# Where the exponential's table is loaded, an empty step among merged work, and the order of the last product's halves

## The chip, the cores and the metric

The kernel runs on one core of a Trainium2 chip. The metric is the device time of one execution in microseconds; lower is better. The core has five engines that run side by side, each with its own list of instructions: TensorE (PE, matrix products; its weight loads are listed as PEld), VectorE (DVE), ScalarE (ACT, the engine that evaluates functions from tables), GpSimd (POOL) and SyncE (SP, which here only issues transfers). ScalarE also issues some transfers; in the profile "SPq" and "ACTq" are those issues.

## The reference

Eight batches; each goes through attention with two separate softmaxes, a two-dimensional Fourier transform of which the real part is added, a layer norm, and a two-layer network, all in float32.

```python
# q, k, v: (8 batches, 8 heads, 576 rows, 64 columns)
q_s = exp(q - max(q, axis=-1)); q_s = q_s / (sum(q_s, axis=-1) + 1e-09)      # over the columns of a head
k_s = exp(k - max(k, axis=2));  k_s = k_s / (sum(k_s, axis=2) + 1e-09)       # over the rows
kv = np.einsum('bhsd,bhse->bhde', k_s, v)
x = np.einsum('bhsd,bhde->bhse', q_s, kv)          # then (B, S, H*D) = (8, 576, 512)

mixed = np.real(fft(fft(x, axis=1), axis=2))
u = x + mixed
un = (u - mean(u)) / np.sqrt(var(u) + 1e-06)
return u + np.maximum(un @ w_ch1, 0.0) @ w_ch2     # w_ch1: 512 x 2048, w_ch2: 2048 x 512
```

## The kernel before

**Groups and orders.** The rows of a batch that aren't handled as its own 512 (64 a batch) are collected over all batches in a ninth "shared" group of 512 rows. The two-layer network runs over the nine groups in the order 0 to 6, 8 (shared), 7. "Order" below means the place in that list, 0 to 8. Order 0 is done by plain products (`plain`). Orders 1 to 8 use Strassen's seven products in place of eight, for the first layer (`up`, L850) and the second (`down`, L886). Each of these is 112 products of 128x128 by 128x256, so 224 main products to an order.

**What runs between the main products.** While the network runs for one group, all the earlier work of the next batch runs in between. `merged(main, side)` deals the side steps out evenly among the main steps:

- Among the `up` of order n: the attention of batch n + 1. `k_exp` takes the maximum (L455, VectorE) and the exponential (L457, ScalarE), `k_turn` transposes on TensorE (L467, L474; copies to `ks` at L468 and L476), `k_times_v` multiplies (L484). `q_exp` does the same for `q` (L519, L521, normalised at L526), `q_turn` and `t_turn` transpose it (L532), `q_times_kv` multiplies (L564), and ScalarE copies the result to `x` (L566 and L581).
- Among the `down` of order n: the Fourier transform of batch n + 1, in four fold steps on VectorE and GpSimd (L603 to L625) and five blocks of products (L655, L658); then two mixing steps for the batch's own rows, a third for the shared rows of a pair of batches when the batch is odd (products L678 and L681, sums into x at L696 and L697); then seven steps of the next group's norm.

**The norm.** Statistics on VectorE (L726, L727), the square root on ScalarE (L730), its reciprocal and the mean's product on VectorE (L731, L732), then four normal rows on ScalarE (L744), each followed by a transpose on TensorE (L750) and a copy to `unT` (L754). ScalarE's tables for the exponential and the square root are different ones, and the program loads one ahead of the first instruction that needs it: exponentials (L457, L521) run in each `up`, the root at the end of each `down`. In orders 6 and 7 there is no attention left.

**Strassen's ends.** A product's result lies in a bank named `ba`, `bb` or `bc`; VectorE sums at L818, L822 and L861, ScalarE applies the relu at L862, GpSimd forms the sums of operands of the second layer from it (L341 to L344). The operands are formed from `unT` in the same way (L348 to L350).

**Weights.** `used(n)` is called behind the last product with a weight block and issues the load of block n + 4 on SP's queue (L392 for the first layer, L394 for the second), so weights stream in with three or four blocks ahead.

**The tail.** In the last group (`last`, order 8) the second layer's last two products, m = 4 and m = 3, are summed by halves: `sums` adds a half of the bank (L903) to x and calls `store`. Half i = 0 is stored through ScalarE's queue, half i = 1 through SP's. A chunk for which the row half and the column half of the group agree (c == u) is stored directly (L935); any other is mirrored, first to a scratch tile in DRAM (L939), then from there in reverse order to the output (L941). For m = 4 the mirrored one is i = 0, for m = 3, the last, it is i = 1.

The instructions of each engine are put in their final order by a scheduler, from the program's order and from what each instruction needs, not by the text alone.

Of the kernel before, what the change touches and what calls it, by code (L numbers as in the profile page):

```python
# [40 lines left out]
F32 = mybir.dt.float32  # L41
I32, U32 = mybir.dt.int32, mybir.dt.uint32
ACT = mybir.ActivationFunctionType
# [3 lines left out]
P = 128  # L47
# [75 lines left out]
class _Block:  # L123
# [466 lines left out]
    def transform(self, b):  # L590


        nc, V, G = self.nc, self.nc.vector, self.nc.gpsimd
        Z = self.work.tile([P, KT, HD], F32, tag="Z", name="Z", bufs=1)
        self.Z[b] = Z
        x = {(c, u): self.xpart(b, c, u) for c in range(2) for u in range(2)}
        eo = {}

        def tokens_folded(some=range(4)):
            for i in some:  # L600
                e, op = ((V if b == 0 else G), ALU.add) if i < 2 else (V, ALU.subtract)
                eo[i] = self.halves()
                e.tensor_tensor(out=eo[i][:, 0:D], in0=x[i % 2, 0], in1=x[i % 2, 1], op=op)  # L603

        def columns_folded(some=range(4)):
            for i in some:
                e, op = ((V if b == 0 else G), ALU.add) if i < 2 else (V, ALU.subtract)
                t = eo[i]
                e.tensor_tensor(out=t[:, 1:HD], in0=t[:, 1:HD], in1=t[:, D - 1:HD:-1], op=op)
                if b == 0:  # L610
                    self.warm(t[:, 0:HD], 2)

        def by_frequency(some=range(4)):

            for i in some:
                e, op = ((G, ALU.add), (G, ALU.subtract), (V, ALU.add), (V, ALU.subtract))[i]
                one, two = eo[i // 2 * 2], eo[i // 2 * 2 + 1]
                (V if b == 0 else e).tensor_tensor(out=eo[i][:, NN:], in0=one[:, 0:NN], in1=two[:, 0:NN], op=op)

        def columns_again(some=(2, 3, 0, 1)):  # L620

            for i in some:
                t, y = eo[i], eo[i][:, NN:]
                V.tensor_tensor(out=t[:, 0:QD], in0=y[:, 0:QD], in1=y[:, HD:QD:-1], op=ALU.subtract)
                V.tensor_tensor(out=y[:, 0:QD], in0=y[:, 0:QD], in1=y[:, HD:QD:-1], op=ALU.add)  # L625

        def at_first():

            for some in ((2, 3), (0, 1)):
                for f in (tokens_folded, columns_folded, by_frequency, columns_again):  # L630
                    f(some)

            t = self.small.tile([P, 1], F32, tag="root", name="root", bufs=1)
            V.tensor_scalar(out=t[:], in0=eo[1][:, NN:NN + 1], scalar1=0.0, scalar2=None, op0=ALU.mult)
            nc.scalar.activation(t[:], t[:], ACT.Sqrt)
            self.wait_for(eo[1][:, NN:], [self.raws[i] for i in range(4)])

        def block(k):


            g = self.live["g", b]
            sines = k in (2, 3)
            own = slice(*{0: (NN, NN + QD), 4: (NN + QD, NN + QD + 1), 1: (0, QD), 2: (NN + 1, NN + QD + 1),
                          3: (1, QD)}[k])
            tail = slice(*{0: (0, QD), 4: (QD, QD + 1), 1: (NN, NN + QD), 2: (1, QD + 1), 3: (NN + 1, NN + QD)}[k])
            n = own.stop - own.start
            if k == KT:

                own, tail = slice(own.start, own.start + P), slice(tail.start, tail.start + P)
            full = self.acc((own.stop - own.start, 512))  # L650
            pz = full[0:n]
            f = sines * NM
            for odd, at, size in ((1, 0, MO), (0, MO, ME)):
                t = eo[3 - odd if sines else odd]
                nc.tensor.matmul(full[:, at:at + size], lhsT=t[:, own], rhs=self.ft[:, f + at:f + at + size], start=at == 0,  # L655
                                 stop=False, skip_group_check=True)
            f += 2 * NM
            nc.tensor.matmul(full[:, 0:NM], lhsT=g[:, tail], rhs=self.ft[:, f:f + NM], start=False, stop=True,  # L658
                             skip_group_check=True)
            z, zt = (self.Zr[0:1], self.ZTr[0:1]) if k == KT else (Z[0:n, k, :], self.ZT[0:n, k, :])  # L660
            nc.scalar.copy(paired(z), interleaved(pz[:, NT - 1:NT - 1 + 2 * ME])[:, 0:P, :])

            at = W * (b % 2)
            nc.scalar.mul(paired(zt[:, at:at + Q]), interleaved(pz[:, 0:2 * MO])[:, 0:NT - 1, ::-1],
                          -1.0 if sines else 1.0)
            nc.scalar.copy(paired(zt[:, at + Q:at + W]), interleaved(pz[:, 0:2 * ME])[:, NT - 2::-1, ::-1])

        folds = [tokens_folded, columns_folded, by_frequency, columns_again] if b else [at_first]
        return folds + [lambda k=k: block(k) for k in (2, 3, 0, 1, 4)]

    def second(self, z, zr, add):

# [43 lines left out]
    def norm(self, g):  # L716

        nc, V = self.nc, self.nc.vector
        mv = self.small.tile([P, 4, 2], F32, tag="mv", name="mv", bufs=2)
        std = self.small.tile([P, 4], F32, tag="std", name="std", bufs=2)  # L720
        unT = self.work.tile([P, 7, 2, HD], F32, tag="unT", name="unT", bufs=1)
        uns = {}

        def stats(i):
            st = self.small.tile([P, 6], F32, tag="st", name="st", bufs=2)
            V.bn_stats(st[:], self.xpart(g, i % 2, i // 2))  # L726
            V.bn_aggr(mv[:, i, :], st[:])  # L727

        def scales(s):
            nc.scalar.activation(std[:, s], mv[:, s, 1], ACT.Sqrt, bias=self.eps[:, 0:1])  # L730
            V.reciprocal(std[:, s], std[:, s])  # L731
            V.scalar_tensor_tensor(out=mv[:, s, 0], in0=mv[:, s, 0], scalar=-1.0, in1=std[:, s], op0=ALU.mult,  # L732
                                   op1=ALU.mult)

        def normal(i):
            un = self.halves()
            x = self.xpart(g, i % 2, i // 2)
            if g == 0:
                V.tensor_scalar(out=un[:, 0:D], in0=x, scalar1=std[:, i:i + 1], scalar2=mv[:, i, 0:1], op0=ALU.mult,
                                op1=ALU.add)  # L740
                if i == 1:
                    self.wait_for(un, [self.raws[i] for i in range(4, 11)])
            else:
                nc.scalar.activation(un[:, 0:D], x, ACT.Identity, bias=mv[:, i, 0:1], scale=std[:, i:i + 1])  # L744
            uns[i] = un

        def turn(i):
            pt = self.turned()
            for k in range(KT):
                nc.tensor.transpose(pt[:, k, :], uns[i][:, k * P:(k + 1) * P], self.ident[:])  # L750

            c, u = i % 2, i // 2
            cols = slice(c * P, (c + 1) * P)
            nc.scalar.copy(unT[:, u:u + 3:2, :, cols], pt[:].rearrange("p (a k) t -> p a k t", a=2))  # L754

        def all_stats():

            for some in ((0, 2), (1, 3)) if g == 0 else (range(4),):
                for i in some:
                    stats(i)  # L760
                scales(slice(some[0], 4, some[1] - some[0]))

        def combine():
            if g > 0:
                self.b_side(lambda i: unT[:, i], lambda i: unT[:, i], V, nc.gpsimd, V)

        return unT, [all_stats] + pipelined((0, 2, 1, 3), [normal, turn]) + [combine]
# [107 lines left out]
    def down(self, g, at):  # L875
        nc, V = self.nc, self.nc.vector
# [3 lines left out]
        def product(m, bank, first, final):  # L880
            n = 15 * at + NP + ORDER.index(m)

            def run(i, q):
                w = self.stream[n]
                for p in range(4 * q, 4 * q + 4):
                    nc.tensor.matmul(bank()[:, i, :], lhsT=h[p][:, A_AT[m], i * P:(i + 1) * P], rhs=w[:, p, :],  # L886
                                     start=first and i == 0 and p == 0, stop=p == NP - 1,
                                     skip_group_check=True)
                if (i, q) == (1, 1):
                    self.used(n)  # L890
                if last and m in (4, 3) and q == 1:
                    sums(m == 4, m != 4, bank(), i)
            return [lambda i=i, q=q: run(i, q) for i in range(2) for q in range(2)]

        def early(i, j, t):
            u, d = i - 1 if (i, j) != (1, 2) else 0, j - 1
# [48 lines left out]
def kernel(ctx: ExitStack, tc: tile.TileContext, q, kT, v, w1, w2, ft,  # L945
# [4 lines left out]
    def front(b, loads=None):  # L950

        first = blk.attention(b, loads)
        steps = late(lambda: blk.transform(b), 9 if b else 6)
        mixes = [lambda c=c: blk.mix_own(b, c) for c in range(2)]
        if b % 2:

# [136 lines left out]
```

## Time and profile before

| what | value |
|---|---|
| median of 8 runs | 1142.64 us (1141.52 to 1145.96) |
| the profiled execution, its own time | 1145.96 us |
| its span | 1144.2 us |
| TensorE's mean granted clock | 0.992 |
| TensorE busy | 1102.2 us, 5472 instructions |
| ScalarE busy | 397.9 us, 956 instructions |
| GpSimd busy | 332.5 us |
| table loads at L457 (exponential) | 7, 1283 ns each |
| table loads at L730 (root) | 7, 1283 ns each |
| other table loads | 2 (L229 at the start, L635 in order 0) |

Times are from the start of the span. Order 0 ends at 204.5 us, orders 1 to 6 at 329.7, 450.5, 574, 694.6, 818.7 and 940, order 7 at about 1046; the last product ends at 1136.9. A line of the timeline gives start, duration, engine, line, operation, output <- inputs, and in brackets how long the engine was idle before it and what it then waited for. Neighbouring instructions of one line are shown as one (x4). One main product is two passes through the array and counts as two instructions.

### The profile page before, as it was taken

The numbers are of one execution on the slowest core, as the hardware profiler recorded it, in microseconds if no ns is written. First come the engines' busy times: TensorE is split into PE (matmuls) and PEld (weight loads), VectorE is DVE, ScalarE is ACT, GpSimd is POOL, SyncE is SP. The second block draws the span as 40 slices with busy tenths as digits, with TensorE's granted clock in tenths as the row PEclk, the third lists the DMA queues.
The fourth block names the chain that finished last, engine by engine and source line by source line (L and its number), as shares of the span: only waits on it lengthen the run. The fifth ranks groups of instructions, "written<-read, shape, count | busy, mean of one in ns | idle before, by whom it ended". The sixth has DMA issues, their size and how long they took to land.

```text
span 1144.2 us, 14639 instructions
## 1 busy us (share of the span) xinstructions
PE 1102.2 (96%) x5472; PEld 922.0 (81%) x5472; DVE 544.3 (48%) x1110; ACT 397.9 (35%) x956; POOL 332.5 (29%) x302
## 2 busy tenths in 40 slices
PE   5799899989999999999999999999999999999997
PEld 5644455878888988888889888788889888888886
DVE  6784766378334734385335633583334352202301
ACT  6585433374133612371226322541234132201200
POOL 2075442235003510324024402261034213302320
PEclk8999999999999999999999999999999999999999
DMA  9377595454346434544356326552454344444451
GB/s 312 116 242 258 210 307 166 137 199 150 106 148 228 180 138 144 182 164 170 129 177 219 148 102 188 180 199 106 143 185 153 111 151 162 183 139 154 150 184 55
DMA packets 92549, 193.79 MB, mean 169 GB/s; under 512 B 23088, under 2 KB 59696, under 8 KB 85312
## 3 DMA queue, kind: packets, MB, share of 16 engines
q1 hardware_dynamic: 90680, 191.82, 49.1%
q10 hardware_dynamic: 1800, 1.05, 0.3%
q8 instruction: 43, 0.70, 0.2%
q14 instruction: 26, 0.21, 0.1%
HBM read 168.72 MB, written 28.31 MB: 172 GB/s over the span
## 4 chain that ended last, share of the span: by engine, by line
PE 79%; DVE 10%; ACT 5%; DMA 3%; issue 1%; POOL 1%; SPq 0%; ACTq 0%; POOLq 0%; DVEq 0%
PE bb L850 13%; PE bb L886 13%; PE bc L886 10%; PE bc L850 9%; PE ba L850 8%; PE ba L886 8%; PE acc L484 3%; PE acc L564 2%; PE bc L789 2%; PE acc L655 2%; PE acc L658 2%; PE tr L467 1%; PE acc L678 1%; PE tr L750 1%; PE tr L532 1%
## 5 line engine op out<-in xcount | busy, mean ns | idle before, releaser
L850 PE MATMUL bb<-unT,big 128*128 128x256 f32 x768 | 188.0, 381 | 0.6 <-DVE u L822 0.6
L886 PE MATMUL bb<-big 128*128 128x256 f32 x768 | 172.8, 379 | 0.0
L850 PEld LDWEIGHTS bb<-unT,big 128*128 128x128 f32 x768 | 142.7, 190 | 24.7 <-DVE u L818 3.4
L886 PEld LDWEIGHTS bb<-big 128*128 128x128 f32 x768 | 145.1, 190 | 20.0
L341 POOL TENSOR_TENSOR big<-big 128x512 f32<-128x512 f32 (+1 forms) x38 | 45.1, 1188 | 310.4 <-ACT big L862 305.7
L850 PE MATMUL bc<-unT,big 128*128 128x256 f32 x512 | 125.2, 379 | 0.0
L850 PE MATMUL ba<-unT,big 128*128 128x256 f32 x512 | 124.3, 379 | 0.0
L862 ACT ACTIVATE big<-big 128x512 f32<-128x512 f32 x96 | 60.3, 628 | 171.0 <-DVE big L861 170.7
L886 PE MATMUL bc<-big 128*128 128x256 f32 x512 | 116.5, 379 | 0.5 <-DVE x L903 0.5
L886 PE MATMUL ba<-big 128*128 128x256 f32 x512 | 114.1, 379 | 0.0
L886 PEld LDWEIGHTS bc<-big 128*128 128x128 f32 x512 | 95.9, 190 | 14.2 <-DVE x L903 0.9
L886 PEld LDWEIGHTS ba<-big 128*128 128x128 f32 x512 | 95.9, 190 | 12.3
L850 PEld LDWEIGHTS bc<-unT,big 128*128 128x128 f32 x512 | 95.5, 190 | 12.5
L850 PEld LDWEIGHTS ba<-unT,big 128*128 128x128 f32 x512 | 95.0, 190 | 11.7
L822 DVE TENSOR_TENSOR u<-bb,s 128x512 f32<-128x512 f32 x40 | 27.6, 690 | 134.8 <-PE bb L886 79.5
L521 ACT ACTIVATE q<-q,qm 128x64 f32<-128x64 f32 x240 | 61.6, 338 | 10.7 <-DVE qm L519 9.9
L349 POOL TENSOR_TENSOR unT<-unT 128x512 f32<-128x512 f32 x8 | 14.2, 1774 | 173.1 <-DVE unT L348 173.1
L818 DVE TENSOR_TENSOR u<-bb,s 128x512 f32<-128x512 f32 x40 | 27.6, 691 | 76.8 <-PE bb L850 38.1
L898 POOL TENSOR_TENSOR x<-x,u 128x512 f32<-128x512 f32 x14 | 17.7, 1268 | 148.6 <-DVE u L822 118.3
L861 DVE TENSOR_TENSOR big<-bc,u 128x512 f32<-128x512 f32 x64 | 44.1, 689 | 26.7 <-PE bc L850 25.9
L814 ACT COPY s<-ba 128x512 f32<-128x512 f32 x40 | 23.4, 584 | 90.0 <-PE ba L886 46.2
L754 ACT COPY unT<-tr 128x512 f32<-128x512 f32 x36 | 20.6, 585 | 86.5 <-PE tr L750 86.0
(221 smaller groups left out, 1665.0 us busy)
## 6 DMA issues: line engine op xcount, KB each, us to landing
big<-w1s SPq DMA_DIRECT2D x64, 896.0 KB
big<-w2s SPq DMA_DIRECT2D x56, 1024.0 KB
big<-in_w_dram SPq DMA_DIRECT2D x21, 512.0 KB
k<-in_kT_dram SPq DMA_DIRECT2D x26, 288.0 KB
q<-in_q_dram SPq DMA_DIRECT2D x27, 256.0 KB
v<-in_v_dram SPq DMA_DIRECT2D x26, 256.0 KB
words<-in_w_dram SPq DMA_DIRECT2D x11, 512.0 KB
w2s<-big SPq DMA_DIRECT2D x8, 512.0 KB
```

The source lines that it names most:

```text
L341: e1.tensor_tensor(out=to(4), in0=at(2), in1=at(3), op=ALU.add)
L484: nc.tensor.matmul(pk, lhsT=ks[:, c, :], rhs=v[:, c, :], start=(c == 0), stop=(c == NC - 1))
L521: nc.scalar.activation(heads[:, h, :], heads[:, h, :], ACT.Exp, bias=m[:, h:h + 1])
L564: nc.tensor.matmul(px[:, r * P:(r + 1) * P], lhsT=qT[:, r, :], rhs=self.kvr[b % 2][:, r, :], start=True, stop=True)
L655: nc.tensor.matmul(full[:, at:at + size], lhsT=t[:, own], rhs=self.ft[:, f + at:f + at + size], start=at == 0, stop=False, skip_group_chec ...
L814: nc.scalar.copy(temp("s1"), box["ba"][:])
L818: V.tensor_tensor(out=temp("u2"), in0=box["bb"][:], in1=box["s1"][:], op=ALU.add)
L822: V.tensor_tensor(out=temp("u3"), in0=box["bb"][:], in1=box["s1"][:], op=ALU.add)
L850: nc.tensor.matmul(bank()[:, i, :], lhsT=w[:, WA_AT[m], k * P:(k + 1) * P], rhs=unT[:, B_AT[m], k, :], start=first and i == 0 and k == 0, ...
L861: V.tensor_tensor(out=hp(i), in0=bank[:], in1=u[:], op=ALU.add)
L862: nc.scalar.activation(hp(i), hp(i), ACT.Relu)
L886: nc.tensor.matmul(bank()[:, i, :], lhsT=h[p][:, A_AT[m], i * P:(i + 1) * P], rhs=w[:, p, :], start=first and i == 0 and p == 0, stop=p == ...
```

## The change

Three edits.

1. In the norms of all groups but the first, behind the root, the reciprocal and the product: a one-column tile `root` gets the exponential of the root's first column (scale 0). Its value isn't used; it is an instruction that needs the exponential's table.
2. Between the four fold steps and the five blocks of the transforms of batches 2 to 7, an empty step. `merged` deals out one step more.
3. In the last product of the last group the halves run in the order 1, 0, so the mirrored chunk is summed and stored first; `used` follows the second of them.

```diff
@@ transform
         folds = [tokens_folded, columns_folded, by_frequency, columns_again] if b else [at_first]
-        return folds + [lambda k=k: block(k) for k in (2, 3, 0, 1, 4)]
+
+        return folds + [lambda: None] * (b > 1) + [lambda k=k: block(k) for k in (2, 3, 0, 1, 4)]
@@ norm, scales
             V.scalar_tensor_tensor(out=mv[:, s, 0], in0=mv[:, s, 0], scalar=-1.0, in1=std[:, s], op0=ALU.mult,
                                    op1=ALU.mult)
+            if g > 0:
+
+                t = self.small.tile([P, 1], F32, tag="root", name="root", bufs=1)
+                nc.scalar.activation(t[:], std[:, 0:1], ACT.Exp, scale=0.0)
@@ down
         def product(m, bank, first, final):
             n = 15 * at + NP + ORDER.index(m)
 
+            order = (1, 0) if last and m == 3 else (0, 1)
+
             def run(i, q):
...
-                if (i, q) == (1, 1):
+                if (i, q) == (order[1], 1):
                     self.used(n)
                 if last and m in (4, 3) and q == 1:
                     sums(m == 4, m != 4, bank(), i)
-            return [lambda i=i, q=q: run(i, q) for i in range(2) for q in range(2)]
+            return [lambda i=i, q=q: run(i, q) for i in order for q in range(2)]
@@ front
-        steps = late(lambda: blk.transform(b), 9 if b else 6)
+        steps = late(lambda: blk.transform(b), (6, 9, 10)[min(b, 2)])
```

## The prediction

> **What bounds the kernel now.** I read the page's busy shares first, then TensorE's list of waits (whole, then stage by stage), then the timeline around the waits that the change can reach.
>
> ```profile
> span 1144.2 us, 14639 instructions
> PE 1102.2 (96%) x5472; PEld 922.0 (81%) x5472; DVE 544.3 (48%) x1110; ACT 397.9 (35%) x956; POOL 332.5 (29%) x302
> ```
>
> TensorE is busy 96% of the span, so only what stops TensorE, or lies behind its last product, can be won or lost. Neither the empty step nor the table loads touch its work: 1102.2 us stay. What stops it (us in total, times, longest):
>
> ```profile
> PE acc L484 <- ACT ks L468: 9.6, 7, 4.1
> PE tr L467 <- ACT k L457: 3.5, 3, 1.5
> PE tr L532 <- DVE q L526: 2.2, 3, 1.3
> ...
> PE acc L655 <- DVE eo L625: 0.7, 2, 0.5
> ```
>
> Taken by stretches of time, all but 0.4 us of L484 falls into order 0 (before 204 us), which has no Strassen stage. From 204 us on the waits are few: L467 1.47 in order 1, 1.04 in each of orders 3 and 5; L532 2.2, all in order 1; L655 0.2 in order 5 and 0.54 in order 6. Orders 2 and 4 show none. One L467 wait in the timeline (start, duration, engine; the bracket is the idle time before it):
>
> ```profile
> 233.03 0.74 DVE L455 TENSOR_REDUCE km<-k 128x1 f32<-128x576 f32 x1
> ...
> 233.15 0.63 ACT L862 ACTIVATE big<-big 128x512 f32<-128x512 f32 x1 [1.10 <-DVE big L861]
> ...
> 233.79 1.28 ACT L457 ACT_TABLE_LOAD   x1
> ...
> 235.09 0.78 ACT L457 ACTIVATE k<-k,km 128x576 f32<-128x576 f32 x1
> ...
> 236.01 0.66 PE L467 MATMUL tr<-ident,k 128*128 128x128 f32 x4 [1.47 <-ACT k L457]
> ```
>
> The maximum is ready at 233.77 and ScalarE is free at 233.78; the load stands between that and the exponential, and TensorE waits for the exponential. Where the load would go instead:
>
> ```profile
> 315.10 0.30 ACT L730 ACTIVATE std<-mv,eps 128x4 f32<-128x4 f32 x1 [4.31 <-DVE mv L727]
> 315.56 0.17 DVE L731 RECIPROCAL std<-std 128x4 f32<-128x4 f32 x1
> 315.76 0.17 DVE L732 SCALAR_TENSOR_TENSOR mv<-mv,std 128x4 f32<-128x4 f32 x1
> 315.96 2.22 ACT L744 ACTIVATE eo<-x,mv,std 128x512 f32<-128x512 f32 x3 [0.56 <-DVE mv L732]
> ...
> 317.56 0.60 PE L750 MATMUL tr<-ident,eo 128*128 128x128 f32 x4
> ```
>
> ScalarE idles only 0.56 us there before the normals (L744) that TensorE's transposes (L750) need. Last, the tail, the queues and sums only:
>
> ```profile
> 1132.67 0.42 DVE L903 TENSOR_TENSOR x<-bc,x 128x256 f32<-128x256 f32 x1 [2.16 <-PE bc L886]
> ...
> 1133.56 0.63 ACTq L941 DMA_DIRECT2D out_dram<-mirror  x1
> 1136.91 0.42 DVE L903 TENSOR_TENSOR x<-bc,x 128x256 f32<-128x256 f32 x1 [3.81 <-PE bc L886]
> 1137.40 0.33 SPq L939 DMA_DIRECT2D mirror<-x  x1
> 1139.11 0.67 SPq L941 DMA_DIRECT2D out_dram<-mirror  x1
> ```
>
> The span ends 5.1 us after the last issue: the last chunk is stored twice in a row, through `mirror`.
>
> **The change part by part.** Besides the text I use the built order of instructions on each engine, before and after. It shows that the scheduler moves far more than the diff does. Places are counted in main products (L850 up, L886 down), 224 to an order; one takes two passes of 0.216 us (3.45 us for 16 passes), so 0.43 us.
>
> *Table loads.* Of seven L457 loads one stays (batch 1); eight loads and eight `root` exponentials come behind the square roots. 16 loads become 19: ScalarE gets 3 × 1.28 + 8 × 0.20 (the `root` row of L229) = 5.5 us more. ScalarE is busy 35%, so the sum costs nothing by itself; the place does. The norms of the last two groups load a table that no later exponential uses, one of them with a second switch behind it.
>
> *Attention in orders 3 and 5.* L467 starts 1.21 us later than TensorE's pace allows (482.15 against 480.08 + 4 × 0.216), the following L484 0.35, the next L467 about 0.3: 1.86 us. Without the load the exponential starts 1.30 us earlier, so the first delay goes. L484 now stands one product nearer to its L467 and waits 0.35 + 0.43 = 0.78 for the copy of `ks`; the next pair moves three products (1.30 us) on and waits no more. Gain 1.86 - 0.78 = 1.08 in each order, 2.1 in both (0 to 3.7).
>
> *Attention in order 1.* L467's delay is 1.63 (236.01 against 233.95 + 2 × 0.216). It moves two products earlier: 1.63 - 1.30 + 0.86 = 1.19 stay, gain 0.44. Four L532 are delayed by 0.77, 0.21, 0.46 and 1.48, in all 2.92. The five L532 move behind by 5, 4, 2, 4 and 6 products (0.9 to 2.6 us), more than each delay; but one load of `q` on SP's queue also moves behind a load of `w2s` (1 MB), and the exponentials of `q` move on ScalarE. If `q`'s chain stays, 2.92 are won; if it moves as far, nothing. I take half, 1.46. Order 1: -1.9 (+0.5 to -3.4; the upper end is that late load of `q`).
>
> *Empty step.* In even orders the first block (L655) moves from product 140 to 144, 1.73 us later; in order 6 it is delayed 0.70 us, behind L625, and that goes: -0.7. Orders 2 and 4 have nothing to win there. In odd orders the first block stays at 144, where the folds on VectorE have only 0.1 to 0.3 us in hand, so I give back 0.5 of the attention's gains there. All later blocks and one to three of the mixes (L678) move by four products.
>
> *Normals.* A load and a `root`, 1.28 + 0.20, stand between square root and normals, with 0.56 us of idle time to swallow them: normals about 1.0 us later in odd orders (0.9 if all the idle time serves, 1.5 if none does), 0.8 in even ones (0.82 idle at 436.07). In odd orders the first transpose moves from product 200 to 207 (3.0 us). In order 1 its slack was 0.8 (317.56 against 315.96 and 0.81 for one normal); 0.8 + 3.0 - 1.0 = 2.8, from which up to 2.4 goes because VectorE now takes an output sum (L911, 0.66) and the mixes' rows, moved by 1.73 us, ahead of the last statistics. It stays above nothing by some 0.3. In even orders the transposes don't move (slack 3.1 in order 2), against 0.8 for the load and 1.7 for the mixes: 0.3 to 0.6 left. So no wait, narrowly. Order 5 waits 0.54 for its first normal today, which I count as 0.3 won (0.5 lost to 0.5 won).
>
> *Borders of the orders.* In orders 1, 3 and 5 the last transpose moves from product 220 to 224, directly ahead of the next order's first product, as in even orders today. There the first `bb` group runs 0.23 us longer, so +0.7 for three. At the end of order 0 normals and transposes move too: +0.2.
>
> *Tail.* The mirrored chunk goes first, its two stores lie under the second half of the product. The last sum (to 1137.33) is then followed by one plain store, L935, on ScalarE's queue. But that queue holds L941 of the product before behind it (today at 1133.56), and that order is unchanged: L935 at 1137.40 takes 0.34, L941 goes at about 1137.8 and needs the same 5.1 us, so the end is at 1142.8: -1.4. With that L941 out of the way it would be about -4; the lower bound is 0.
>
> Sum: -2.1 - 1.9 + 0.5 - 0.7 - 0.3 + 0.7 + 0.2 - 1.4 = -5.0 us. The profiled execution took 1145.96 (span 1144.2, 1.8 around it), the slowest of the eight shown; it would go to 1141.0. Taken from their median, 1142.64, it gives 1137.6.
>
> *A rule against it.* The trace shows 1.28 us for a load, with 0.02 us on either side of it. The Trainium skill ("ScalarE: Activation LUTs", "What ACT_TABLE_LOAD costs") puts a drain of about 1.38 us to each load, about 2.66 for a switch, and its rules ask for fewer switches, where this change makes three more. By that price, an estimate, normals would be 1.4 us later than above, and six orders would wait some 0.9 us each, 5 to 6 in all, which would take the whole gain.
>
> **The rivals.**
>
> *The folds keep the gains (chance 0.17).* What attention wins is lost again at the first block of orders 1, 3 and 5, since VectorE's folds set its start. For it: L655 waits for L625 in order 5 already. Against: the folds start from sums that TensorE's L564 feeds, so they come earlier too. Left: tail -1.4, order 6 -0.7, borders +0.9, order 5 -0.3: -1.5, 1141.1.
>
> *Normals late (0.15; the slower side).* Square root and normals slip past the slack of 0.3 to 0.6, at the first transposes of orders 1 to 6: VectorE runs one more row of a mix (0.74 + 0.15 + 0.42 + 0.42 = 1.73, the rows at 432.42 to 433.89) ahead of the last statistics than I placed. Price 6 × (1.73 - 0.45) = 7.7, so 1145.3. It outweighs the rest when normals come 0.45 + 5.0 / 6 = 1.3 us later than worked out. For it: the slack is thin and VectorE's order is the scheduler's. Against: VectorE is idle for much of these stretches and the built order shows the rows that I counted.
>
> *All waits go (0.08).* Order 1 wins 3.4, orders 3 and 5 all 3.7, the folds follow: 3.6 more, 1134.0. Against: L484 behind its own L467.
>
> **How the numbers follow.** The forecast has 0.60. Faster means by over 0.2% (2.3 us, about what a measurement of this kernel can tell from no change): nearly all of the forecast (0.57), all of the last rival (0.08), a little of the first (0.02): 0.67. Same: most of the first rival, a little of the forecast and of the second: 0.20. Slower: the second, 0.13. The forecast's own range is 1136.1 to 1140.0, with order 1 at its bounds (1.5 down, 2.4 up). The range given reaches down to the third rival and up past the first, 1134.0 to 1142.2, and leaves out the second and a little below.
>
> **What would show it.** L467's waits on `k` after 204 us gone in orders 3 and 5, near 1 us in order 1; L484 waiting 0.8 us in orders 3 and 5; L532's waits under 1.5 us; L655's gone in order 6; no L750 wait on L744 above 0.5; the last issue an L941 on ScalarE's queue at 5 us before the end. Wrong would be: L750 in the list of waits with several us, new waits at L655 in odd orders, or at `bb` L850 behind a border.

## The result and the profile after

The changed kernel takes 1138.1 us (median of 14 runs, 1135.5 to 1143.46) against 1143.01 us before (38 runs, 1141.43 to 1146.02): a ratio of 0.9957, 95% interval 0.9948 to 0.9966, so 4.9 us faster. Its profiled execution took 1141.34 us with a span of 1139.5. The forecast was 5.0 us. That the sum came out so close is partly luck: three of its terms were right to a tenth of a microsecond, the two largest were too large by about 2.5 together, and what I had given back to the folds was a gain. The sections below take them apart.

Lines below the edits are shifted: the up products are L855 now (L850 before), the down products L893 (L886), the root L731 (L730), the table load and exponential behind it L738, normals L749 (L744), their transposes L755 (L750), the last sums L910 (L903), the stores L942, L946 and L948 (L935, L939, L941).

First TensorE's waits over the whole changed run (us in total, times, longest):

```profile
PE acc L484 <- ACT ks L468: 9.3, 6, 3.5
...
PE tr L532 <- DVE q L526: 3.9, 3, 2.0
...
PE tr L467 <- ACT k L457: 1.1, 1, 1.1
...
PE tr L532 <- PE bb L855: 0.6, 1, 0.6
PE bc L893 <- DVE x L910: 0.5, 1, 0.5
...
PE tr L532 <- DVE T L554: 0.5, 1, 0.5
```

L467's waits fell from three to one, L655's on the folds are gone, and the wait on L749's normals is gone too. But L532's waits on q rose from 2.2 to 3.9, where the prediction had named under 1.5 as a sign of being right. Order 3's attention shows the intended part (start, duration, engine, line; the bracket is idle time):

```profile
478.29 0.74 DVE L455 TENSOR_REDUCE km<-k 128x1 f32<-128x576 f32 x1
...
478.41 0.63 ACT L867 ACTIVATE big<-big 128x512 f32<-128x512 f32 x1 [1.10 <-DVE big L866]
479.07 0.78 ACT L457 ACTIVATE k<-k,km 128x576 f32<-128x576 f32 x1
...
480.07 0.60 PE L467 MATMUL tr<-ident,k 128*128 128x128 f32 x4
...
481.40 1.27 PE L484 MATMUL acc<-v,ks 128*128 128x128 f32 x9 [0.62 <-ACT ks L468]
```

The exponential follows the relu at once, and L467 has no bracket: its wait is gone. L484 pays in part, as it stands right behind L467 now. The load is here instead (norm at the end of order 1):

```profile
315.14 0.30 ACT L731 ACTIVATE std<-mv,eps 128x4 f32<-128x4 f32 x1 [3.73 <-DVE mv L728]
315.45 1.28 ACT L738 ACT_TABLE_LOAD   x1
...
316.75 0.20 ACT L738 ACTIVATE root<-std 128x1 f32<-128x1 f32 x1
316.86 2.21 ACT L749 ACTIVATE eo<-x,mv,std 128x512 f32<-128x512 f32 x3
319.47 0.60 PE L755 MATMUL tr<-ident,eo 128*128 128x128 f32 x4
```

From the root's start to the first normal it is 1.72 us, before 0.86. The first normal ends near 317.66 (316.86 and 0.80), 1.8 us ahead of its transpose. The tail, sums and queues:

```profile
1129.45 0.42 DVE L910 TENSOR_TENSOR x<-bc,x 128x256 f32<-128x256 f32 x1 [2.17 <-PE bc L893]
...
1131.65 0.67 SPq L948 DMA_DIRECT2D out_dram<-mirror  x1
1133.69 0.42 DVE L910 TENSOR_TENSOR x<-bc,x 128x256 f32<-128x256 f32 x1 [3.81 <-PE bc L893]
1134.19 0.34 ACTq L942 DMA_DIRECT2D out_dram<-x  x1
1134.58 0.63 ACTq L948 DMA_DIRECT2D out_dram<-mirror  x1
```

The last issue is the mirrored store of the product before, on ScalarE's queue behind the plain one. The span, 1139.54, ends 5.0 us after it, and 5.85 us after the last sum's start (before: 1144.16 - 1136.91 = 7.25).

The table lists how long each up and each down took in the profiled executions, from the start of its first main product to that of the next part. "Untouched" is the third experiment below, whose instructions before the last product are those of the kernel before; it shows which differences are scatter. Orders 7 and 8 and the downs of orders 2 and 4 are the same in all, to 0.02 us. (Order 7 ends at 1039.2 us before, not at 1046.)

| part | before | untouched | after | after - before | exponential alone | empty step alone |
|---|---|---|---|---|---|---|
| order 0 ends at | 204.49 | 200.02 | 203.90 | -0.59 | 203.44 | 200.24 |
| order 1 up | 67.93 | 68.04 | 67.44 | -0.49 | 67.43 | 67.91 |
| order 1 down | 57.26 | 57.25 | 57.23 | -0.03 | 57.23 | 57.25 |
| order 2 up | 62.35 | 62.35 | 62.59 | +0.24 | 62.35 | 62.58 |
| order 3 up | 66.16 | 65.32 | 66.15 | -0.01 | 64.86 | 65.43 |
| order 3 down | 57.23 | 57.62 | 57.23 | 0.00 | 57.24 | 57.52 |
| order 4 up | 62.35 | 62.35 | 62.59 | +0.24 | 62.35 | 62.59 |
| order 5 up | 65.88 | 65.46 | 64.85 | -1.03 | 64.81 | 65.68 |
| order 5 down | 58.24 | 58.11 | 57.23 | -1.00 | 57.23 | 57.63 |
| order 6 up | 62.35 | 62.35 | 62.59 | +0.24 | 62.35 | 62.59 |
| order 6 down | 59.12 | 59.13 | 58.35 | -0.77 | 59.13 | 58.35 |
| last sum's start to the end | 7.25 | 5.70 | 5.85 | -1.40 | 7.21 | 7.23 |

The column of differences adds up to -4.6, the two spans' difference. Two entries are mostly scatter rather than effect. Order 0 ends anywhere from 200.0 to 204.5 us in these executions, with nearly the same work: over the whole of it TensorE's granted clock was 0.97 in the run of before, 0.99 in the untouched one, 0.97 after, and TensorE was busy for 178.4, 174.9 and 178.6 us. And order 3's up took 66.16 before with a wait (0.6) of a `bb` product on L822 that the two other runs of the same instructions there don't have (65.3 and 65.4), and 66.15 after with a wait of L532 that is usually shorter (the fourth experiment and the last).

### The profile page after: what moved, and what is told of

Read it like the earlier page. It is cut to its first block, busy times and chain, and to the rows that moved or that the text cites. A ratio compares the mean times of both kernels' runs of the same rounds, so it can differ in the third digit from the quotient of the medians.

```text
span 1139.5 us, 14646 instructions
## 1 busy us (share of the span) xinstructions
PE 1100.6 (97%) x5472; PEld 920.5 (81%) x5472; DVE 543.3 (48%) x1110; ACT 402.6 (35%) x967; POOL 332.1 (29%) x302
## 3 DMA queue, kind: packets, MB, share of 16 engines
q10 hardware_dynamic: 1800, 1.05, 0.3%
## 4 chain that ended last, share of the span: by engine, by line
PE 86%; DVE 6%; ACT 3%; DMA 2%; issue 2%; POOL 1%; SPq 0%; ACTq 0%; POOLq 0%; DVEq 0%
PE bb L893 15%; PE bb L855 14%; PE bc L893 10%; PE ba L893 10%; PE bc L855 9%; PE ba L855 9%; PE acc L484 3%; PE acc L564 2%; PE bc L794 2%; PE acc L655 2%; PE acc L658 2%; PE acc L679 1%; PE tr L532 1%; PE tr L755 1%; PE tr L467 1%
## 5 line engine op out<-in xcount | busy, mean ns | idle before, releaser
L855 PE MATMUL bb<-unT,big 128*128 128x256 f32 x768 | 187.9, 381 | 0.0
L893 PE MATMUL bb<-big 128*128 128x256 f32 x768 | 172.1, 379 | 0.0
L893 PEld LDWEIGHTS bb<-big 128*128 128x128 f32 x768 | 145.4, 190 | 20.3
L855 PEld LDWEIGHTS bb<-unT,big 128*128 128x128 f32 x768 | 142.6, 190 | 23.0 <-DVE u L823 2.7
L341 POOL TENSOR_TENSOR big<-big 128x512 f32<-128x512 f32 (+1 forms) x38 | 45.5, 1198 | 284.8 <-ACT big L867 279.2
L855 PE MATMUL bc<-unT,big 128*128 128x256 f32 x512 | 125.8, 379 | 0.0
L855 PE MATMUL ba<-unT,big 128*128 128x256 f32 x512 | 123.9, 379 | 0.0
L893 PE MATMUL bc<-big 128*128 128x256 f32 x512 | 116.0, 379 | 0.5 <-DVE x L910 0.5
L893 PE MATMUL ba<-big 128*128 128x256 f32 x512 | 114.6, 379 | 0.0
L893 PEld LDWEIGHTS bc<-big 128*128 128x128 f32 x512 | 96.1, 190 | 14.3 <-DVE x L910 0.9
L893 PEld LDWEIGHTS ba<-big 128*128 128x128 f32 x512 | 95.7, 190 | 12.1
L855 PEld LDWEIGHTS bc<-unT,big 128*128 128x128 f32 x512 | 95.1, 190 | 12.6
L855 PEld LDWEIGHTS ba<-unT,big 128*128 128x128 f32 x512 | 94.9, 190 | 11.7
L661 ACT COPY Z<-acc 128x256 f32<-128x256 f32 (+1 forms) x32 | 12.0, 375 | 107.2 <-PE acc L658 107.1
```

Of the source, the lines that this page charges most:

```text
L341: e1.tensor_tensor(out=to(4), in0=at(2), in1=at(3), op=ALU.add)
L855: nc.tensor.matmul(bank()[:, i, :], lhsT=w[:, WA_AT[m], k * P:(k + 1) * P], rhs=unT[:, B_AT[m], k, :], start=first and i == 0 and k == 0, ...
```

## The experiments

The first four are from one chip: three take the change apart, each the kernel before with one edit, and the fourth tests what L532 waits for.

**The exponential alone.**

```diff
@@ norm, on the kernel before
+            if g > 0:
+                t = self.small.tile([P, 1], F32, tag="root", name="root", bufs=1)
+                nc.scalar.activation(t[:], std[:, 0:1], ACT.Exp, scale=0.0)
```

> Before plus the exponential behind the root alone. Theory A (the parts act apart, each where the built order moves something): the up of order 5 about 1.0 us shorter, that of order 1 about 0.5, that of order 3 about 0.0, because there a new wait of L532 on q (2.0 us) takes back what L467 and the bb wait on u lose; order 5's down some 0.4 shorter (first transpose 3 products later); orders 2, 4 and 6 as before, with no wait at L750. In all -1.9 to -2.6 us against before, about 1140.7. Rival B (the exponential's gain needs the empty step, because the folds set the first blocks of odd orders): the ups gain the same, but the downs of orders 1, 3 and 5 give it back at L655, in all -0.5 or less. Rival C (normals late): waits at L750 on L744 in several orders and a time above before.

Measured: 1141.78 us, ratio 0.9986 (0.9973 to 0.9998). The ups of orders 1, 3 and 5 are 0.6, 0.5 and 0.65 us shorter than in the untouched run, and the downs of orders 3 and 5 don't give it back, they are 0.4 and 0.9 shorter. So rival B fell: with the attention earlier the folds are earlier too, and the waits of L655 go in orders 3 and 5 without the empty step (in order 6 it stays, 0.70). No transpose waits for a normal from order 1 on: rival C fell. (At the end of order 0 the last transpose waits 0.24 us for a copy, L759, as in the changed kernel; see below.) The border products of orders 2, 4 and 6 are unchanged at 62.35.

**The empty step alone.**

```diff
@@ transform, on the kernel before
-        return folds + [lambda k=k: block(k) for k in (2, 3, 0, 1, 4)]
+        return folds + [lambda: None] * (b > 1) + [lambda k=k: block(k) for k in (2, 3, 0, 1, 4)]
@@ front
-        steps = late(lambda: blk.transform(b), 9 if b else 6)
+        steps = late(lambda: blk.transform(b), (6, 9, 10)[min(b, 2)])
```

> Before plus the empty step alone. Theory A: attention unchanged (L467 1.47, 1.04, 1.04 and L532 2.2 as before); the first block of order 6 loses its wait (-0.77), the first transpose of order 5 its 0.54; the ups of orders 2, 4 and 6 each 0.24 longer at the border, since the last transpose then stands directly ahead of them: in all about -0.6 to -1.0 us, 1142.2. Rival B: the empty step is what gives the down of order 5 its whole 1.0 us (the wait of L655 on the folds too) and the ups some of theirs: -2 or more.

Measured: 1141.71 us, ratio 0.9993 (0.9981 to 1.0005), by itself not told from no change. Its parts are as theory A has them: order 6's down 0.78 shorter, order 5's down 0.5 shorter (the transpose's wait gone, L655's 0.32 still there), and 0.24 lost at each of three borders. By itself the empty step thus earns 1.3 us and gives 0.7 back. In the whole change it earns less: order 5's down is as short with the exponential alone (57.23), so 0.8 of order 6 stands against 0.7 at the borders.

**The swapped halves alone.**

```diff
@@ down, on the kernel before
+            order = (1, 0) if last and m == 3 else (0, 1)
...
-            return [lambda i=i, q=q: run(i, q) for i in range(2) for q in range(2)]
+            return [lambda i=i, q=q: run(i, q) for i in order for q in range(2)]
```

> Before plus the swapped halves of the last product alone. Everything to the last product as before; the distance from the last sum's start to the end of the span falls from 7.3 to 5.8 us: -1.5 us, about 1141.5. Rival: the last chunk's store was not what ended the span, and the time stays within 0.3 us.

Measured: 1142.44 us, ratio 0.999 (0.9979 to 1.0002), by itself not told from no change. From the last sum's start to the end it took 5.70 us, 1.55 less than before. The medians of the three parts lie 1.2, 1.3 and 0.6 us under the 1143.01 of their 30 runs of before, together 3.1, each uncertain by about 1.4; the parts of the profiles add up to -3.0 - 0.5 - 1.5 = -5.0 against the untouched stages. That agrees with parts that act apart, with one exception: order 5's down, which the first two shorten by 0.9 and 0.5, is only 0.9 shorter with both.

**L532's new wait: a maximum that nobody needs yet.** In the changed kernel's order 3, VectorE and what it holds up:

```profile
495.88 0.75 DVE L455 TENSOR_REDUCE km<-k 128x1 f32<-128x576 f32 x1 [2.05 <-DMA k<-in_kT_dram]
...
497.15 0.67 DVE L523 TENSOR_REDUCE qrec<-q 128x8 f32<-128x512 f32 x1
...
498.33 0.97 DVE L524 TENSOR_SCALAR qrec<-qrec 128x8 f32<-128x8 f32 x1
...
499.57 1.59 DVE L526 TENSOR_TENSOR q<-q,qrec 128x512 f32<-128x512 f32 x1
...
501.22 0.66 PE L532 MATMUL tr<-ident,q 128*128 128x128 f32 x4 [2.01 <-DVE q L526]
```

L455 there belongs to the next batch: the scheduler takes its first two k tiles ahead of time, though L467 needs them only in the next order. It did so before too, but then q's sum (L523) stood between the two maxima (L455 at 491.86 and 495.17, L523 at 493.85); now it stands behind both. So VectorE sits 2.05 us for k's transfer ahead of q's sum, and L532 waits 2.01. To move these maxima, one element of each of the two k tiles is combined, by two small operations, with a result that exists only at the end of the up:

```diff
@@ k_exp, on the changed kernel
         m = self.small.tile([P, 1], F32, tag="km", name="km", bufs=3)
+        _, b, r = it
+        if b > 1 and b % 2 and r < 2:
+            self.wait_for(self.xshared(b // 2), [k.bitcast(I32)])
         V.reduce_max(m[:], k, axis=AX.X, negate=True)
```

> The changed kernel, with two one-element operations on VectorE that keep the maxima (L455) of the next odd batch's first two k tiles behind the shared rows' result (L581) of the order before. In the changed kernel these maxima, which nobody needs until the next order, stand among q's work on VectorE and wait there for k's transfer (2.05 us at 495.88). Theory D: that wait is what makes L532 wait for q in orders 3 and 5 (2.17 and 0.85 us later than TensorE's pace) and part of it in order 1 (1.34): without it the ups of orders 3 and 5 get 2.2 and 0.85 us shorter, order 1 up to 1.3, in all -3 to -4 us against the changed kernel, about 1134.5. Rival E: ScalarE's exponentials of q (L521), in between relu and copies, are late by themselves: L532's waits stay, and the time stays within 0.7 us of the changed kernel.

Measured: 1137.64 us, ratio 0.995 (0.9932 to 0.9967). The ups of orders 3 and 5 took 64.02 and 64.00, with one wait left in either stretch (waits of this run from 451 to 574 us; L487 is L484 there):

```profile
PE acc L487 <- ACT ks L471: 0.6, 1, 0.6
```

So what theory D forecast for orders 3 and 5 came: 0.8 us each against the usual 64.8, and 2.1 in the execution in which k came late. That the wait for k is the whole cause isn't shown. In order 5 of the changed kernel a second wait, for a product, stands between that maximum and q's sum, and then the normalisation (L526) takes 1.42 us:

```profile
739.10 0.75 DVE L455 TENSOR_REDUCE km<-k 128x1 f32<-128x576 f32 x1 [0.96 <-DMA k<-in_kT_dram]
740.51 0.69 DVE L866 TENSOR_TENSOR big<-bc,u 128x512 f32<-128x512 f32 x1 [0.66 <-PE bc L855]
...
742.74 1.42 DVE L526 TENSOR_TENSOR q<-q,qrec 128x512 f32<-128x512 f32 x1
```

Holding the maxima takes away both: in orders 3 and 5 q's sum moves ahead of that sum of the up, and the normalisation takes 0.69, since it starts before GpSimd's work (the last section says what GpSimd has to do with it). In order 1 the theory fails: the up took 67.88 in place of 67.44, and one L532 came 1.81 us late. There the transposes stand up to three products earlier than in the changed kernel, and VectorE waits for ScalarE's exponentials of q, as rival E has it (L526 is q's sum in this run, L529 the normalisation):

```profile
252.68 0.69 DVE L526 TENSOR_REDUCE qrec<-q 128x8 f32<-128x512 f32 x1 [1.30 <-ACT q L524]
...
254.82 1.59 DVE L529 TENSOR_TENSOR q<-q,qrec 128x512 f32<-128x512 f32 x1
```

The time as a whole fell by 0.5 us, not by the 3 to 4 expected, and by itself isn't told from the changed kernel's.

The next four are from another chip.

**The tail's queues swapped.** Nothing is left behind the last plain store.

```diff
@@ store, on the changed kernel
-        e = nc.sync if d is None or c else nc.scalar
+        e = nc.sync if d is None or (c == 1) != ((u, d) == (0, 1)) else nc.scalar
```

> The changed kernel, with the last product's two halves stored through the other queues: the mirrored half (m = 3, i = 1) through ScalarE's, the last, plain half through SP's, where nothing stands behind it. Theory F: after the change the span ends with the mirrored store of m = 4 (L948), queued on ScalarE behind the last plain store, 5.8 us after the last sum's start. With nothing behind the plain store the end comes some 3.4 us after the last sum's start: -2.4 us against the changed kernel, about 1135.7. Rival: a plain store issued that late ends the span at nearly the same time, and less than 0.8 us is won.

Measured: 1137.41 us, ratio 0.9953 (0.994 to 0.9966). Its profiled tail, by sums and queues:

```profile
1129.54 0.42 DVE L910 TENSOR_TENSOR x<-bc,x 128x256 f32<-128x256 f32 x1 [2.17 <-PE bc L893]
...
1130.40 2.02 ACTq L948 DMA_DIRECT2D out_dram<-mirror  x2
1133.77 0.42 DVE L910 TENSOR_TENSOR x<-bc,x 128x256 f32<-128x256 f32 x1 [3.81 <-PE bc L893]
```

Both mirrored stores are issued by 1132.4, ahead of the last sum. The span, 1137.4, ends 3.6 us after its start, not 5.85: 2.2 us won, and the queue was the cause. The median shows 0.7 of it, in five runs, which the scatter of order 0 covers; the combined run below shows the rest.

**Two more loads in each norm.**

```diff
@@ norm, on the changed kernel
                 nc.scalar.activation(t[:], std[:, 0:1], ACT.Exp, scale=0.0)
+                nc.scalar.activation(t[:], t[:], ACT.Sqrt)
+                nc.scalar.activation(t[:], t[:], ACT.Exp, scale=0.0)
```

> The changed kernel with one more root and one more exponential of the same one-column tile behind the first, so two more table loads ahead of the normals in each norm but the first. Theory G (a load costs 1.28 us and a one-column activation 0.20, nothing else): normals come 2 x 1.48 = 2.96 us later, more than the 1.5 to 1.8 us that the first transposes of orders 1 to 4 have in hand in the changed kernel; so L750's line waits about 1.2 us in orders 1 and 3, 1.5 in orders 2 and 4, some 1.4 at the end of order 0, nothing in order 6, and the time is 4 to 7 us above the changed kernel's, 1142 to 1145: the slower side of the prediction, reached. Rival H (a drain of 1.4 us goes with each load): normals come some 5.7 us later, and the time is 15 us or more above. Rival I: the built order moves transposes away, and the time rises by less than 2 us.

Measured: 1144.24 us, ratio 1.0015 (1.0003 to 1.0027), 6.1 us above the changed kernel's median. The size is what theory G forecast, which is luck, since the place isn't. ScalarE and the transposes at the end of order 0 (L751 are the normals, L757 the transposes):

```profile
193.20 0.30 ACT L731 ACTIVATE std<-mv,eps 128x4 f32<-128x4 f32 x1 [1.74 <-DVE mv L728]
193.51 1.28 ACT L738 ACT_TABLE_LOAD   x1
...
194.81 0.20 ACT L738 ACTIVATE root<-std 128x1 f32<-128x1 f32 x1
194.92 0.80 ACT L751 ACTIVATE eo<-x,mv,std 128x512 f32<-128x512 f32 x1
195.73 1.28 ACT L739 ACT_TABLE_LOAD   x1
...
198.50 1.28 ACT L740 ACT_TABLE_LOAD   x1
199.79 0.20 ACT L740 ACTIVATE root<-root 128x1 f32<-128x1 f32 x1
199.90 1.50 ACT L751 ACTIVATE eo<-x,mv,std 128x512 f32<-128x512 f32 x2
...
200.75 1.36 PE L757 MATMUL tr<-ident,eo 128*128 128x128 f32 x8 [2.02 <-ACT eo L751]
```

The built order puts the added loads behind the first normal, so that one isn't later and the slack at the first transposes wasn't tried. The other normals come 5 us after it and TensorE waits 2.7 us there (2.02 and 0.68; 0.24 in the changed kernel). In orders 2 and 4 the down grew by only 0.08, and in order 6 by nothing. Order 1's up is 0.9 longer: right behind these waits, up to 206 us, its first passes ran at a granted clock of 0.50, where the changed kernel has 1.00. Order 5's is 1.4 longer, by one wait (1.19) for a VectorE sum, L829, ahead of which VectorE had waited 1.51 for a transfer of q. That the loads are the cause of either isn't shown. Rival H fell: each of the added loads took 1.28 us and began within 0.02 us of the end of the instruction before it. Rival I fell too, by the time.

**No load where no exponential follows.**

```diff
@@ norm, on the changed kernel
-            if g > 0:
+            if 0 < g < B - 1:
```

> The changed kernel without the exponential in the last two norms (groups 8 and 7), behind which no exponential follows. Their normals are ready 5 to 90 us ahead of their transposes in the changed kernel, so the three loads less win nothing: within 0.5 us of the changed kernel; every part of every order as long as there. Rival: ScalarE's list is shorter in order 6 and its down, 58.35 us, gets shorter by 0.3 or more.

Measured: 1138.61 us, ratio 0.9961 (0.995 to 0.9972). Every part of every order as after, to 0.04 us, but for order 3's up, 64.81, its usual length. In the parts the needless loads cost nothing.

**Held maxima and swapped queues together.** The two edits above on the changed kernel.

> The changed kernel with the held maxima of the run on L455 and the swapped queues of the tail together. If both act apart: orders 3 and 5 as in the first (64.0 us of up each), the end some 3.4 us behind the last sum's start: about 4.5 to 5 us below the changed kernel, 1133.3. If the tail's stores meet nothing else, its part is the same as alone.

Measured: 1135.15 us, ratio 0.993 (0.9915 to 0.9945). Orders 3 and 5 took 63.99 of up, the end came 1134.8 - 1131.03 = 3.8 us after the last sum's start: both act apart. The median fell by 3.0 us from the changed kernel's, less than the 4.5 to 5 expected, with order 1's 0.45 lost.

Last, a fitted version and the changed kernel once more, both from a third chip.

```diff
@@ on the run before: k_exp, transform, front
-        if b > 1 and b % 2 and r < 2:
+        if b > 3 and b % 2 and r < 2:
...
-        return folds + [lambda: None] * (b > 1) + [lambda k=k: block(k) for k in (2, 3, 0, 1, 4)]
+        return folds + [lambda: None] * (b == B - 1) + [lambda k=k: block(k) for k in (2, 3, 0, 1, 4)]
...
-        steps = late(lambda: blk.transform(b), (6, 9, 10)[min(b, 2)])
+        steps = late(lambda: blk.transform(b), 6 if b == 0 else 9 + (b == B - 1))
```

> The changed kernel with the swapped queues of the tail, the held maxima for batches 5 and 7 alone (not 3), and the empty step in batch 7's transform alone. If the border's 0.24 us comes from the last transpose standing directly ahead of the next order (product 224 in place of 220) and not from the table load, the ups of orders 2, 4 and 6 go back to 62.35 (0.24 less each); order 1's up back to 67.43 (held: 67.9); orders 3 and 5 stay at 64.0; order 6's down stays at 58.35, since only batch 7's transform runs there; orders 1, 3 and 5's downs stay at 57.23 if the first transposes, which stand at product 202 and 204 in place of 207 and 208, still find their normals. In all 1.2 us less than the run with both held and swapped, about 1134.0. Rival: with the transposes earlier, normals come too late in orders 1, 3 and 5 behind root, load and exponential, and L750's line waits 0.5 or more in each: no gain.

Measured: 1134.82 us, ratio 0.9929 (0.9917 to 0.9941), the lowest median of the study. Its ups of orders 2, 4 and 6 took 62.35, order 1's 67.44, those of orders 3 and 5 63.99 and 64.02, order 6's down 58.35, those of orders 1, 3 and 5 57.24. No normal was late; the first transposes had 0.8 us in hand in orders 1, 3 and 5. From order 1's first product to the last it took 926.1 us, 1.1 less than the run before: the 0.24 at the border belongs to the last transpose's place, not to the load, as the exponential alone (62.35) and the empty step alone (62.59) had shown. The medians of the two differ by less, 0.3 us, in five runs each on two chips.

> The changed kernel itself, once more, beside the fitted one. From order 1's first product to the last, the same lengths of every up and down within 0.1 us, but for order 3's up, which had 64.8 to 66.4 with the same instructions, by when k's transfer lands; the time within 1 us of 1138.1, the rest of the scatter before 204 us.

Measured: 1139.08 us, ratio 0.9969 (0.9958 to 0.998), a little less gain than the result above. Every part as after to 0.04 us, but for order 3's up, 64.85, which has 0.84 of late L532 in place of 2.17. So the usual effect in orders 3 and 5 is a wait of 0.85 us. The two executions of order 3 differ by little at first: counted from the order's start, k's maximum begins 0.31 us later in the one with 2.17. The other 1.0 comes behind it, where L524 and L526 took 0.97 and 1.59 us in place of 0.16 and 1.40.

## Why the prediction came out right, point by point

*What held.* L467's and L484's places were worked out to a tenth: L467 gone in orders 3 and 5, 1.21 us late in order 1 (worked out: 1.19), L484 0.78 late (0.78). Order 6's first block gave 0.77 (0.7), the borders cost 0.72 (0.7), the tail gave 1.40 (1.4), with the L948 on ScalarE's queue as the last issue. The table's price was the trace's 1.28 us. The 2.66 us that the Trainium skill ("ScalarE: Activation LUTs", "What ACT_TABLE_LOAD costs") gives for a switch don't show here: the load began 0.02 us after the root's end and ended 0.01 us before the next activation.

*Order 1: -1.9 forecast, -0.5 measured.* The step that failed is the half that I gave to q. L532 was late by 2.92 us in all before and by 2.85 after (0.12 + 0.65 + 1.34 + 0.74): its transposes moved behind by up to six products, and q's chain moved as far: in both kernels each of the four started only 0.06 to 0.26 us after the end of q's normalisation (L526). My lower bound, "nothing", was the answer; the 0.44 of L467 is all that was won.

*Orders 3 and 5: -2.1 forecast.* The mechanism held, and 1.87 us of delays in each became 0.78 at L484. But the sum took that gain for the whole effect, and about 0.85 us of late L532 came back in each, since q's sum now stands behind the maximum of the next batch on VectorE. The prediction named that nowhere: it looked at who waits on ScalarE and TensorE, and not at what stands ahead of q in VectorE's new order. Short pauses of the up's own products behind the attention (0.25 us in each order of the untouched run) went as well. Net, by the exponential alone, 0.5 and 0.65 against the untouched run.

*Folds and order 5: +0.5 and -0.3 forecast, about -1.0 measured in order 5's down.* I gave back half a microsecond to the folds; instead the wait of L655 in order 5 (0.32) went, because attention was earlier, and the first normal's wait (0.54) went whole. The first rival, which lived on this step, was refuted by the exponential alone.

*Normals.* They moved by 0.86 in orders 1 and 3 and 0.6 in even ones (forecast 1.0 and 0.8). The slack left at the first transposes was 1.5 to 1.8 us, not 0.3 to 0.6: I had counted the mixes' rows fully against it. The second rival was thus farther off than its price said. It is only partly tested: the doubled loads were put elsewhere, and showed 2.7 us of waiting at the end of order 0, so the slower side is real but lies beyond this change.

*The end of order 0: +0.2 forecast.* It is there in the changed kernel and in the exponential alone, and not in the untouched run:

```profile
203.40 0.66 PE L755 MATMUL tr<-ident,eo 128*128 128x128 f32 x4 [0.24 <-ACT unT L759]
```

In the time it is hidden by scatter: order 0's end moves by up to 4.5 us from one execution to the next, of which 3.5 between the run of before and the untouched one is busy time of TensorE.

Together: order 1's and q's losses (1.4 and 1.1 us less than forecast) were made up by the folds and order 5 (1.2 better) and by order 0 (0.8 better, which is scatter, as its own step cost 0.24). The sum was right because these errors had opposite signs.

## What to carry to other kernels

Moving work off the instruction that TensorE waits for helps only until the next one in the chain is late: read the new order of every engine that feeds the chain, and look above all for an instruction ahead of it that waits for a transfer and that nobody needs yet. At the end of a program the store of the last sum need not be the last issue: what counts is what else is queued behind it. On top of the swap (1.4 to 1.55 us), moving the two-step stores to a queue of their own won another 2.2. Compare profiles part by part; here most parts repeat to 0.04 us while whole runs scatter by several.

## What the runs showed of the hardware

Some of VectorE's instructions stretch where GpSimd works at the same time. In the changed kernel's order 3 the normalisation of q (L526) took 1.59 us at 499.57, while its median is 0.69. GpSimd's L342 began 0.22 us before it:

```profile
499.35 1.26 POOL L342 TENSOR_TENSOR big<-big 128x512 f32<-128x512 f32 x1
...
499.57 1.59 DVE L526 TENSOR_TENSOR q<-q,qrec 128x512 f32<-128x512 f32 x1
500.57 1.72 POOL L343 TENSOR_TENSOR big<-big 128x512 f32<-128x512 f32 x1
```

GpSimd isn't always slowed: L342 took its usual 1.26 us beside it, but L343, which began while it still ran, 1.72. The small L524, 0.16 us at 495.04 before, took 0.97 at 498.33 with L341 running. Over the whole changed kernel, L526 took 0.68 or 0.69 us wherever GpSimd was idle, and 1.42 to 1.74 where GpSimd worked beside it for over 1 us. Not every instruction is so: the sum L523 and the maximum L519 took 0.63 to 0.69 us beside GpSimd as without it.

This was seen and not tested by a run of its own. In the changed kernel it adds up to 1.05 us to q's chain at L526, and up to 0.8 at L524. Where q has time in hand, as with the held maxima in orders 3 and 5, nothing waits for it. Where q hasn't, it is about as large as the wait: 0.73 of the 0.85 us in the changed kernel's order 5, and 0.9 ahead of the latest L532 of order 1, which came 1.48 us late in the kernel before, 1.34 in the changed one and 1.81 with held maxima. Whether those waits would go if GpSimd's work stood elsewhere, no run here tells.
